# Seven products in the first layer of four more token blocks, with moved scores, state copies and buffers, in a fused retention and feed-forward kernel

## The chip, the cores and the metric

The kernel runs on one core of one Trainium2 chip. The metric is the device time of one execution in microseconds (us); lower is better. The engines are named as in the profile: PE is TensorE, which multiplies matrices (PEld is its loading of weights), DVE is VectorE, ACT is ScalarE, POOL is GpSimd, and SP is the engine whose queue issues most of the DMAs.

## The reference

Eight batches of eight heads go through a retention layer (attention without softmax, with a decay per head); the heads' results are laid side by side to 4608 tokens of 512 features, and these go through two matrix products with a gelu between.

```python
# q, k, v: (8, 8, 576, 64)
scores = scale * np.matmul(q, k.transpose(0, 1, 3, 2))
gamma = 1.0 - 2.0 ** (-5.0 - np.arange(H))
Dmat = np.where(rel >= 0, gamma[:, None, None] ** rel, 0.0)      # rel = i - j
attn = np.matmul(scores * Dmat, v)
x = attn.transpose(0, 2, 1, 3).reshape(4608, 512)
h = x @ w_in                                                     # w_in: 512 x 2048
g = 0.5 * h * (1.0 + np.tanh(c * (h + 0.044715 * h * h * h)))
out = g @ w_out                                                  # w_out: 2048 x 512
```

## The kernel before

**Tiling.** The tokens are worked in nine blocks `t` = 0 to 8 of 512. Blocks 0 to 7 hold the first 512 positions of batch `t`; the last 64 positions of all batches (the tails) are block 8. While block `t` goes through the two layers, the attention of batch `t + 1` is computed between its matmuls, and the batch after that is loaded, cast and transposed. Everything that the matmuls read is 16-bit.

**The first layer** (`up`, L465) makes one chunk of 128 of the 2048 hidden features for 512 tokens: four matmuls 512 columns wide into a PSUM bank `hp`, and a gelu on ACT into `gT`. Sixteen chunks make a block. In the last two blocks (`WIN`, L501) three quarters of the chunks are computed in another way (`up_prod`, L541): a group `j` is two chunks of the lower half of the features and two of the upper half, and its 2 x 2 block product is made by the Strassen-Winograd scheme with seven products of half the size instead of eight. One product is four matmuls 256 columns wide. Products 1, 6, 7 and 4 accumulate in one bank (`hB`), 2 has `hA`, 5 and 3 accumulate in `hC`. Where a bank's content is needed before the next product is added to it, it is copied out or read first: ACT copies it after product 1 (tile `ws`, the variable `s`) and after 6 (`wv`), DVE after 7 (`wu`), and DVE adds `hA` or `hC` to these tiles. Gelus of what results are put off by one step (`due`). The scheme needs sums of the weights (`in_sums`, L505, DVE: 4 operations per group, once) and sums of the inputs (`x_sums`, L522, DVE: 4 operations per block).

**The second layer** is made by the same scheme in all blocks but the first (`prod`, L651, and `after`, L673): seven products in the order 1, 6, 5, 7, 2, 4, 3 (another order in the last two blocks), each in two halves of 8 matmuls. Products 1 and 2 use bank A, 6, 7 and 4 accumulate in bank B, 5 and 3 in bank C. After 6, DVE adds bank B to ACT's copy of product 1 (`keep["u2"]`, tile `k2`); after 7 it makes `u3`; both are in the profile as `k<-k,opB` at L680. The activation sums that the products need (`act_sums`, L637, DVE: s1, s2, a difference written in place over `gT`, s4) are made pair by pair as soon as gelu has delivered two chunks of each half.

**Attention beside a block.** `scores` (L901) computes the scores of two 128-token chunks (tiles `st`) and multiplies them by a mask on DVE (`masks`, L383, tiles `ret`). `outs` (L912) multiplies them by the values, adds what the state of the earlier chunks gives (`past`, from the tiles `tbd`, `tbt`), and computes the next chunks' state products (`state`). `later` (L757) is the running state: two DVE operations (`scan`: `vs`, `ws`) and two copies of 64x256 each into `tbd` (`spread`, L425), on ACT. In blocks 2, 4, 6 and 7 the tails of two batches are worked along (`TP`).

**Order.** Every engine works its own queue in the order in which the program issues. What lies beside the matmuls is put at a step by hand: `at(t, u, f)` runs `f` after step `u` of block `t`; steps 0 to 15 are the first layer, 16 to 29 the halves of the seven products. From step 16 on GpSimd casts the next batch but one (`cc`, four `k` and four `q`; ACT casts `v`, but GpSimd for batch 3), after a small copy (`gate`, L953) that waits for the block's last activation sum. When the casts are done, SP issues two DMA transposes (`turn_dma`). Loads are held back from step 16 (`hold`) to step 29 (`resume`).

**Buffers.** All loads go into a ring of 16 buffers of 2 KB per partition (`LD`, `lds`); a load may be issued when a cast has freed a buffer (`pump`). The sums of the last blocks use the same ring when the loads are over.

The eight PSUM banks are handed out first in, first out (`bank`, `drop`).

Of the kernel before, what the change touches and what calls it, by code (L numbers as in the profile page):

```python
# [20 lines left out]
def kernel(  # L21
# [23 lines left out]
    LD = 16  # L45
# [24 lines left out]
    def lds():  # L70
        return sb.tile([128, 512], F32, tag="ld", name="ld", bufs=LD)

# [54 lines left out]
    seq += [("o", f) for f in FO[:LATE]]  # L127
    TP = {2: 0, 4: 2, 6: 4, 7: 6}
    seq += body(1)[:6] + [("o", f) for f in FO[LATE:]] + body(1)[6:]
    for b in range(1, B):  # L130
        seq += body(b) if b > 1 else []
        if b - 1 in TP:
            seq.append(("t", TP[b - 1]))
    q_ld = {"next": 0, "free": LD, "hold": False}

    def pump(freed=0):
        q_ld["free"] += freed
        while q_ld["next"] < len(seq) and not q_ld["hold"]:
            s = seq[q_ld["next"]]
            if s[0] != "t":  # L140
                if q_ld["free"] == 0:
                    return
                q_ld["free"] -= 1
            q_ld["next"] += 1
            {"b": load, "i": load_w_in, "o": load_w_out, "t": load_tails}[s[0]](*s[1:])
# [101 lines left out]
    def cast(b, key, c, eng):  # L247
        a = att[b]
        raw = a["raw"].pop((key, c))
        dst = a[key][:, 512 * c : 512 * c + 512]  # L250
# [250 lines left out]
    WIN = {t: 3 for t in (NTB - 2, NTB - 1)}  # L501
    GW = max(WIN.values())
    wi = {}

    def in_sums(j, ns):  # L505
        if not wi:
            for g in range(0, GW, 2):
                for n in "234":
                    wi[n, g // 2] = sb.tile([128, 2, 512], F16, tag="ld", name="wi" + n, bufs=LD)
# [10 lines left out]
    xw = {}  # L520

    def x_sums(t):  # L522
        if not xw:
            for n in ("12", "34"):
                x = sb.tile([128, 2, 4, 2, TL], F16, tag="ld", name="x" + n, bufs=LD)
                xw[int(n[0])], xw[int(n[1])] = x[:, 0], x[:, 1]
            for n in range(3):
                for s in "svu" if n < 2 else "vu":
                    wk[s, n] = sb.tile([128, 512], F32, tag="ld", name="w" + s, bufs=LD)
# [9 lines left out]
    wk, wb, due = {}, {}, []  # L539

    def up_prod(t, j, m):  # L541
# [23 lines left out]
        s, v, u3 = wk["s", j % 2], wk["v", j % 3], wk["u", j % 3]  # L565
# [56 lines left out]
    wt = {n: const.tile([128, NH, HD], F16, name="wt" + n) for n in "1234"}  # L622
    W11, W12 = w_out_sb[:, 0:NH, 0:HD], w_out_sb[:, 0:NH, HD:DM]
    W21, W22 = w_out_sb[:, NH:NF, 0:HD], w_out_sb[:, NH:NF, HD:DM]

# [11 lines left out]
    def act_sums(t, f0, f1, us=slice(0, 2), parts=(0, 1)):  # L637
# [6 lines left out]
        if 0 in parts:  # L644
            nc.vector.tensor_tensor(out=s["1"], in0=a21, in1=a22, op=ALU.add)  # L645
            nc.vector.tensor_tensor(out=s["2"], in0=s["1"], in1=a11, op=ALU.subtract)
            nc.vector.tensor_tensor(out=a21, in0=a11, in1=a21, op=ALU.subtract)
        if 1 in parts:
            nc.vector.tensor_tensor(out=s["4"], in0=a12, in1=s["2"], op=ALU.subtract)  # L649

    def prod(t, m, u):  # L651
# [7 lines left out]
        tag = {1: "A", 2: "A", 3: "C", 4: "D" if t in WIN else "B", 5: "C", 6: "B", 7: "B"}[m]  # L659
        if t in WIN and m == 3:  # L660
# [12 lines left out]
    def after(t, m, u):  # L673
        last = t == NTB - 1
        if u == 0 and not (last and m == 3 or t in WIN and m == 4) or u == 1 and t in WIN and m == 4:
            return
# [4 lines left out]
        def send(o, i):  # L681
# [5 lines left out]
            for v in range(2):  # L687
                end(o[:, v], i, v)
        def end(o, i, v, d=slice(0, DM)):
            b = 4 * v + 2 * i  # L690
            for h, e in enumerate((nc.sync, nc.scalar)):
                r0 = S * (b + h) + M0
                e.dma_start(out=out[r0 : r0 + TL, d], in_=o[TL * h : TL * h + TL, d])
# [3 lines left out]
        elif m == 6:  # L697
            keep["u2"] = sb.tile([128, 2, HD], F32, tag="k2", name="k2", bufs=1)
            add(keep["u2"], keep["s1"], pr("B"))
            for f in range(0, NH if t in WIN else 0, 2):  # L700
                act_sums(t, f, f + 2, parts=(1,))
        elif m == 7:
# [4 lines left out]
            drop(op.pop("B")) if t in WIN else None  # L707
            drop(op.pop("C")) if t in WIN else None
        elif m == 2:
# [3 lines left out]
            for v in range(2 if last else 0):  # L713
                end(keep["o0"][:, v], 0, v, slice(0, HD))
        elif m == 5 and t in WIN:
# [4 lines left out]
        elif m == 3:  # L720
            x = "E" if t in WIN else "C"
# [3 lines left out]
        elif m == 4 and t in WIN:  # L725
# [10 lines left out]
    def cast_w(kind, *i):  # L736
        src = w_raw.pop((kind,) + i)
        if kind == "i":
# [7 lines left out]
        pump(1)  # L746
# [6 lines left out]
    def cc(b, key, c, eng):  # L753
        cast(b, key, c, eng)
        pump(1)
# [4 lines left out]
    def later(b, c):  # L760
        scan(b, c)
        spread(b, c, A.copy)
# [57 lines left out]
    def run(t, u, last=False):  # L820
# [3 lines left out]
    W_ORDER = (  # L824
        "01 02 05 11 06 12 p 15 07 16 21 22 p 04 25 17 03 26 14 p 13 27 p Q0 24 a0 23 a1 Q1 a3 a2"
    ).replace("p", "").split(" ")
    for n in range(GW):
        at(NTB - 3, 17 + 2 * n, lambda n=n: in_sums(n, (3, 2)))
        at(NTB - 3, 18 + 2 * n, lambda n=n: in_sums(n, (4, 1)))
    at(NTB - 3, 27, lambda: x_sums(NTB - 2))  # L830
    at(NTB - 2, 17, lambda: x_sums(NTB - 1))


    at(0, -12, lambda: [V.memset(x, 0.0) for x in (tbd[1][:, 1:], *tbt[1:])])
    for n, f in enumerate(FO):
        at(0, -5 + n // 4 if n < LATE else 6, lambda f=f: cast_w("o", f))
        if 8 <= n < LATE:
# [47 lines left out]
    at(1, 12, lambda: weight_sums(4, (0, 3), V))  # L885
# [42 lines left out]
    for c in range(2):  # L928
        at(2, c, lambda c=c: later(nb, c))
    for t in range(2, B):  # L930
        b, tl = t + 1, TP.get(t)
        s0, o0, s1, o1 = 9, 15, 19, 25
# [5 lines left out]
        at(t, o0 + 1, lambda b=b: later(b, 2))  # L938
        at(t, o1, lambda t=t, nb=b + 1: outs(t, 2, None, (nb, 0, 1) if nb < B else None))
        at(t, o1 + 1, lambda b=b: later(b, 3))  # L940
        if b + 1 < B:
            for c in range(2):
                at(t + 1, c, lambda c=c, nb=b + 1: later(nb, c))
# [113 lines left out]
```

## Time and profile before

| | |
|---|---|
| median of 3 runs | 296.68 us (296.66 to 296.77) |
| the profiled execution | 296.39 us, its span 294.7 us, granted clock 0.997 |
| block 2, start to start on PE | 87.06 to 117.61 us |
| block 3 | 117.61 to 147.49 |
| block 4 | 147.49 to 178.05 |
| block 5 | 178.05 to 207.92 |
| block 6 | 207.92 to 238.38 |
| block 7 (three groups as seven products) | 238.38 to 264.35 |
| block 8 (likewise) | 264.35 to about 290 |

Times within the profile are from the start of the span. The page's first part gives each engine's busy time; the windows give it by stretch of time, so that an engine which is free on average can be seen to be full in one stage. A row of the timeline is: start, duration, engine, source line, operation, tile written and tiles read, shape and count; a bracket at its end says how long the engine had been idle and who released it.

These rows of the busiest groups are the prices of what the change moves or adds:

```profile
L561 PE MATMUL hC<-x,w_in_sb 128*128 128x256 f16 x48 | 7.2, 273 | 0.0
L568 DVE TENSOR_TENSOR ws<-ws,hA 128x512 f32<-128x512 f32 x6 | 4.1, 689 | 5.2 <-ACT ws L581 5.1
L581 ACT COPY ws<-hB 128x512 f32<-128x512 f32 x6 | 3.4, 574 | 9.6 <-PE hB L561 9.6
L537 DVE TENSOR_TENSOR x<-xT 128x512 f16<-128x512 f16 x4 | 1.7, 418 | 0.0
L745 POOL CAST w_in_sb<-ld 128x512 f16<-128x512 f32 x16 | 9.9, 629 | 2.1 <-DMA ld<-in_moe_w_in_dram 1.5
```

The columns are: count, busy time in us, mean ns of one, and the idle time before them with what ended it. Matmuls are pipelined, so that the step from one start to the next is shorter than a duration.

### The profile page before, as it was taken

How to read it: one execution, taken by the hardware profiler on the slowest of the kernel's cores; microseconds unless marked ns; L12 is line 12 of the kernel's file. 1: busy time of each engine (PE TensorE's matmuls, PEld its weight loads, DVE VectorE, ACT ScalarE, POOL GpSimd, SP SyncE). 2: the span in 40 equal slices, each digit the busy share in tenths (PEclk: the TensorE clock that was granted, in tenths of full speed). 3: DMA queues.
4: the chain of work that ended last, by engine and by line, in shares of the span. 5: the costliest groups of instructions: out<-in, count | busy, mean ns of one | idle time of the engine just before them, and what ended most of it. 6: DMA issues, size and time to landing. Idle time of an engine off the chain costs nothing. (4 is left out here: it accounts for less than half of the span.)

```text
span 294.7 us, 7531 instructions
## 1 busy us (share of the span) xinstructions
PE 282.2 (96%) x3100; PEld 204.3 (69%) x3100; DVE 191.7 (65%) x396; ACT 168.4 (57%) x313; POOL 100.2 (34%) x133
## 2 busy tenths in 40 slices
PE   6779999999999999999999999999999999999993
PEld 2458745888884588448844885478547887887782
DVE  6790606789754873477448654855488968974863
ACT  5377443998239663866386736664666258507800
POOL 4587487960880082007700640059030000000000
PEclk9999999999999999999999999999999999999998
DMA  7999999999969998999899949944941030003013
GB/s 202 307 357 372 341 317 292 280 280 211 194 165 232 216 225 169 261 214 194 103 271 221 169 88 273 211 109 76 263 93 38 0 145 1 2 20 125 1 38 107
DMA packets 129058, 52.92 MB, mean 180 GB/s; under 512 B 101632, under 2 KB 120576, under 8 KB 129024
## 3 DMA queue, kind: packets, MB, share of 16 engines
q1 hardware_dynamic: 128544, 51.92, 74.5%
q8 instruction: 24, 0.39, 0.6%
q10 hardware_dynamic: 480, 0.52, 0.6%
q14 instruction: 10, 0.08, 0.1%
HBM read 36.70 MB, written 9.44 MB: 157 GB/s over the span
## 5 line engine op out<-in xcount | busy, mean ns | idle before, releaser
L471 PE MATMUL hp<-xT,w_in_sb 128*128 128x512 f16 x352 | 79.0, 379 | 0.0
L477 ACT ACTIVATE gT<-hp 128x512 f16<-128x512 f32 x88 | 50.6, 597 | 31.0 <-PE hp L471 30.4
L471 PEld LDWEIGHTS <-w_in_sb 128*128 128x128 f16 x352 | 34.0, 98 | 38.2
L666 PEld LDWEIGHTS <-gT 128*128 128x128 f16 x512 | 49.0, 98 | 7.2 <-issue 0.5
L666 PEld LDWEIGHTS <-s 128*128 128x128 f16 x384 | 37.1, 98 | 4.8
L645 DVE TENSOR_TENSOR s<-gT 128x512 f16<-128x512 f16 x32 | 14.4, 449 | 28.0 <-ACT gT L477 27.0
L953 POOL COPY gate<-s 128x1 f16<-128x1 f16 x5 | 0.9, 190 | 90.7 <-DVE s L649 90.7
L489 PE MATMUL hp<-xT,w_in_sb 128*128 128x256 f16 x256 | 30.3, 273 | 1.1 <-POOL w_in_sb L745 0.9
L666 PE MATMUL opA<-w_out_sb,gT 128*128 128x256 f16 x256 | 31.0, 273 | 0.1
L425 ACT CAST tbd<-ws 64x256 f16<-64x256 f32 x48 | 19.4, 405 | 16.0 <-DVE ws L416 15.4
L489 PEld LDWEIGHTS <-w_in_sb 128*128 128x128 f16 x256 | 24.5, 98 | 4.9 <-POOL w_in_sb L745 1.6
L666 PE MATMUL opB<-wt,gT 128*128 128x256 f16 x224 | 26.9, 273 | 0.1
L383 DVE TENSOR_TENSOR ret<-st,cm 128x512 f16<-128x512 f32 x40 | 24.8, 681 | 0.0
L266 POOL TENSOR_TENSOR cq<-ld,sc 128x512 f16<-128x512 f32 x20 | 21.7, 1086 | 0.0
L460 ACT CAST xT<-xs 128x512 f16<-128x512 f32 x36 | 19.3, 592 | 3.3 <-PE xs L450 1.8
L266 POOL TENSOR_TENSOR ck<-ld,sc 128x512 f16<-128x512 f32 x20 | 21.0, 1050 | 0.0
L495 ACT ACTIVATE gT<-hp 128x512 f16<-128x512 f32 x32 | 18.5, 602 | 3.8 <-PE hp L489 3.5
L680 DVE TENSOR_TENSOR k<-k,opB 128x512 f32<-128x512 f32 x16 | 11.0, 687 | 14.2 <-ACT k L696 7.5
L711 ACT COPY ost<-opA 128x512 f32<-128x512 f32 x8 | 4.7, 586 | 24.1 <-PE opA L666 17.5
L293 ACT COPY tt<-tr 128x1024 f16<-128x1024 f16 (+1 forms) x12 | 11.8, 998 | 10.8 <-PE tr L287 10.7
L416 DVE TENSOR_TENSOR ws<-vs,gt 128x256 f32<-128x256 f32 x24 | 15.7, 654 | 1.1
L666 PE MATMUL opC<-wt,s 128*128 128x256 f16 x128 | 15.5, 273 | 0.0
(124 smaller groups left out, 440.0 us busy)
## 6 DMA issues: line engine op xcount, KB each, us to landing
ld<-in_q_dram SPq DMA_DIRECT2D x32, 256.0 KB, 5.3
ld<-in_k_dram SPq DMA_DIRECT2D x32, 256.0 KB, 5.3
ld<-in_v_dram SPq DMA_DIRECT2D x32, 256.0 KB, 5.4
out_dram<-ost SPq DMA_DIRECT2D x16, 512.0 KB, 3.8
ld<-in_moe_w_in_dram SPq DMA_DIRECT2D x16, 256.0 KB, 5.9
ld<-in_moe_w_out_dram SPq DMA_DIRECT2D x16, 256.0 KB, 5.3
lt<-in_k_dram SPq DMA_DIRECT2D x8, 128.0 KB, 5.4
lt<-in_q_dram SPq DMA_DIRECT2D x8, 128.0 KB, 4.3
```

The lines of the kernel that those rows point to most:

```text
L266: eng.tensor_tensor(out=dst.rearrange("p (h d) -> p h d", d=D), in0=raw.rearrange("p (h d) -> p h d", d=D), in1=sc[:, s0].unsqueeze(2).to_ ...
L293: cp(out=o, in_=t)
L383: nc.vector.tensor_tensor(out=r.rearrange("p (n i) -> p n i", i=128), in0=t.rearrange("p (n i) -> p n i", i=128), in1=(cm if b < PAIR else ...
L416: nc.vector.tensor_tensor(out=w, in0=uc, in1=gt, op=ALU.mult)
L425: cp(out=(tbd[b % 2][r, c, :, r] if c < NC - 1 else tbt[b % NT4][r, :, r]), in_=w[r])
L460: nc.scalar.copy(out=xT[:, g0 : g0 + 2], in_=xs.rearrange("p (n g t) -> p g n t", n=HP, g=2))
L471: nc.tensor.matmul(hp.rearrange("p (g t) -> p g t", t=TL), w_in_sb[:, ct, 128 * fc : 128 * fc + 128], xT[:, o : o + TB // TL, ct, :], star ...
L477: nc.scalar.activation(out=gT[t][:, fc].rearrange("p i n -> p (i n)"), in_=hp, func=AF.Gelu_apprx_tanh)
L489: nc.tensor.matmul(hp[:, 256 * x : 256 * x + 256].rearrange("p (g t) -> p g t", t=TL), w_in_sb[:, ct, 128 * (f + x) : 128 * (f + x) + 128] ...
L495: nc.scalar.activation(out=gT[t][:, f : f + 2, 2 * u : 2 * u + 2, :].rearrange("p f i n -> p f (i n)"), in_=hp.rearrange("p (f n) -> p f n ...
L645: nc.vector.tensor_tensor(out=s["1"], in0=a21, in1=a22, op=ALU.add)
L666: nc.tensor.matmul(op[tag][:, HD * u : HD * u + HD], lhs(f), rhs[:, f], start=(new and f == 0), stop=(f == NH - 1), skip_group_check=True,)
```

## The change

Seven things change together.

1. Blocks 3 to 6 compute groups 0 and 1 (half of the first layer) as seven products; the other eight chunks stay plain. The order within the block is written out (`p` is a plain chunk, `01` is product 1 of group 0, and so on), and the activation sums come in two runs at its end: `a` is s1 and s2, `b` the difference in place and s4.
2. In these blocks the first scores move from step 9 to 11, the outputs from 15 to 17, the second scores from 19 to 20, the second outputs from 25 to 26.
3. From batch 3 on, the state copies are made by GpSimd.
4. The weight sums of groups 0 and 1 move from block 6 to block 2 (steps 17, 18, 21, 22), those of group 2 to step 24 of block 6; the x sums are made at step 28 of the block before (block 8: step 17, as before).
5. The ring has 19 buffers. Seven of them, kept back when batch 2 has been issued, hold the sums; 12 remain for the loads. Some temporaries share the tiles `k1` to `k3` with the second layer.
6. One sum of the second layer's weights (`wt["1"]`) is written in place, and its first half moves from block 0 to step 14 of block 1.
7. The last block's stores of two halves of a result are joined to one DMA per queue.

```diff
-    LD = 16
+    LD = 19
+    KEPT = 7
...
+        if b == NPE - 1:
+            seq += [("keep",)] * KEPT
...
+            if s[0] == "keep":
+                kept.append(ring.popleft())
...
-    WIN = {t: 3 for t in (NTB - 2, NTB - 1)}
+    FIN = (NTB - 2, NTB - 1)
+    WIN = {t: 3 if t in FIN else 2 for t in range(NPE, NTB)}
...
+    def hold(shape, dt):
+        n = kept.pop() if kept else ring.popleft()
+        return sb.tile(list(shape), dt, tag=f"ld{n}", name="wk", bufs=1)
...
+    def temp(t, j, s):
+
+        m = j % (2 if s == "s" else 3)
+        if s == "s" and t not in FIN or m == 0:
+            return sb.tile([128, 512], F32, tag={"s": "k1", "v": "k2", "u": "k3"}[s], name="w" + s, bufs=1)
+        if (s, m) not in wk:
+            wk[s, m] = hold((128, 512), F32)
+        return wk[s, m]
...
-    def act_sums(t, f0, f1, us=slice(0, 2), parts=(0, 1)):
+    def act_sums(t, f0, f1, us=slice(0, 2), parts=(0, 1, 2)):
...
             nc.vector.tensor_tensor(out=s["2"], in0=s["1"], in1=a11, op=ALU.subtract)
+        if 1 in parts:
             nc.vector.tensor_tensor(out=a21, in0=a11, in1=a21, op=ALU.subtract)
-        if 1 in parts:
+        if 2 in parts:
             nc.vector.tensor_tensor(out=s["4"], in0=a12, in1=s["2"], op=ALU.subtract)
...
-            for v in range(2):
-                end(o[:, v], i, v)
...
             for h, e in enumerate((nc.sync, nc.scalar)):
-                r0 = S * (b + h) + M0
-                e.dma_start(out=out[r0 : r0 + TL, d], in_=o[TL * h : TL * h + TL, d])
+                e.dma_start(out=rows(2 * i + h, slice(0, 2), d), in_=o[TL * h : TL * h + TL, :, d])
...
-    def later(b, c):
+    def later(b, c, cp=A.copy):
         scan(b, c)
-        spread(b, c, A.copy)
+        spread(b, c, cp)
...
+    W_ORDER = {
+        2: "p 01 02 05 p 06 11 12 p 07 15 16 04 p 03 17 p 14 13 p p p a0 a1 a2 a3 b0 b1 b2 b3",
+        3: "01 02 05 11 06 12 p 15 07 16 21 22 p 04 25 17 03 26 14 p 13 27 p Q0 24 c0 23 c1 Q1 c3 c2",
+    }
+    for j, (t, u) in enumerate([(NPE - 1, 17), (NPE - 1, 21), (NTB - 3, 24)]):
+        at(t, u, lambda j=j: in_sums(j, (3, 2)))
+        at(t, u if t > NPE else u + 1, lambda j=j: in_sums(j, (4, 1)))
+    for t in WIN:
+        at(t - 1, 17 if t == NTB - 1 else 28, lambda t=t: x_sums(t))
...
-        if 8 <= n < LATE:
+        if 9 <= n < LATE:
...
-    at(1, 12, lambda: weight_sums(4, (0, 3), V))
+    at(1, 12, lambda: weight_sums(4, (3, 0), V))
+    at(1, 14, lambda: weight_sums(0, [0], V))
...
-        s0, o0, s1, o1 = 9, 15, 19, 25
+        s0, o0, s1, o1 = (11, 17, 20, 26) if t in WIN and t not in FIN else (9, 15, 19, 25)
...
-        at(t, o0 + 1, lambda b=b: later(b, 2))
+        at(t, o0 + 1, lambda b=b: later(b, 2, P.tensor_copy))
...
-        at(t, o1 + 1, lambda b=b: later(b, 3))
+        at(t, o1 + 1, lambda b=b: later(b, 3, P.tensor_copy))
...
-            todo = deque(f + h for f in range(2 * WIN.get(t, 0), NH) for h in (0, NH))
+            todo = deque([4, 12, 5, 13, 6, 7, 14, 15][4 * (WIN.get(t, 2) - 2) :])
```

## The prediction, made before the changed kernel was built or run

> **What bounds the kernel now.** I read the page first, then the busy time by block, then the waits, then the order of time around the places that the change touches.
>
> ```profile
> PE 282.2 (96%) x3100; PEld 204.3 (69%) x3100; DVE 191.7 (65%) x396; ACT 168.4 (57%) x313; POOL 100.2 (34%) x133
> ```
>
> TensorE is the bound: 282.2 of 294.7 us, and the rest is the start and the last stores. So what the change takes from TensorE counts in full, and what it adds elsewhere costs only where TensorE has to wait. The windows by block show who is near that point.
>
> ```profile
> core 0: us, PE busy (x) PEld busy (x) DVE busy (x) ACT busy (x) POOL busy (x), PEclk, DMA share, GB/s
> 87.00:117.60 30.60, 30.60 (x311) 20.98 (x309) 18.93 (x38) 18.75 (x36) 9.04 (x10) 1.00 1.03 214
> 117.60:147.50 29.90, 29.90 (x287) 20.20 (x286) 17.83 (x36) 17.84 (x34) 10.58 (x11) 1.00 0.97 192
> 207.90:238.40 30.50, 30.41 (x295) 20.68 (x294) 24.20 (x53) 16.68 (x32) 2.50 (x2) 1.00 0.34 84
> ```
>
> These are blocks 2, 3 and 6. VectorE has 12 us to spare in block 3 and 6 in block 6, where the weight sums lie today. In block 6 it was late once:
>
> ```profile
> 234.15 0.68 DVE L680 TENSOR_TENSOR k<-k,opB 128x512 f32<-128x512 f32 x1
> ...
> 234.89 1.91 PE opB L666 x16
> ```
>
> (The second line is from the chain of waits.) Product 4 accumulates on top of 6 and 7 in bank B, so it may start only when VectorE has read the bank; TensorE started 0.06 us after the read ended. The same holds for product 7 after the u2 sum of product 6. In block 3 this hand-over has slack:
>
> ```profile
> 134.06 0.42 DVE L649 TENSOR_TENSOR s<-gT,s 128x512 f16<-128x512 f16 x1
> 134.39 0.42 DVE L413 TENSOR_TENSOR vs<-us,ws 128x256 f32<-128x256 f32 x1
> 134.60 0.19 POOL L953 COPY gate<-s 128x1 f16<-128x1 f16 x1 [21.96 <-DVE s L649]
> 134.84 1.23 DVE L416 TENSOR_TENSOR ws<-vs,gt 128x256 f32<-128x256 f32 x1
> 137.57 0.69 DVE L680 TENSOR_TENSOR k<-k,opB 128x512 f32<-128x512 f32 x1 [1.50 <-ACT k L696]
> ...
> 139.13 1.91 PE L666 MATMUL opB<-wt,gT 128*128 128x256 f16 x16
> ```
>
> The u2 sum ends at 138.26 and product 7 starts at 139.13: 0.87 us of slack. The reader should also see that ws took 1.23 us and not 0.43: it waited for the GpSimd cast that started at 134.75.
>
> **The change, part by part.** *Seven products.* A 512-column matmul group of 4 goes every 0.865 us (24 matmuls from 126.90 to 132.09), a product of 4 matmuls of 256 columns every 0.4375 us (block 7). One group of columns costs 4 x 0.865 = 3.46 us today and 7 x 0.4375 = 3.06 us as products: 0.40 us less. Two groups in each of four blocks: **-3.2 us**.
>
> What VectorE gets for it, per group: sum of s, copy and sum of u, sum of v, 4 x 0.69 = 2.75 us, and per block 4 sums of x at 0.35 to 0.42 us, 1.6 us: 7.1 us per block. By amount it fits block 3 (17.8 + 7.1 of 29.9) and block 6 barely (24.2 + 5.5 - 3.3 for the eight weight sums that leave). By place it does not, and this is my main term. In the new order all eight pairs of activation sums, which lie between the gelus today, come in one run after the scores' masks and ahead of the scan and of the u2 sum. Take T = 0 at block 3's first matmul. Five plain chunks and 13 products: the scores start at 5 x 0.865 + 13 x 0.4375 = 10.0. TensorE then has scores 0.56, one product 0.44, three chunks 2.6, products 1, 6 and 5 at 1.76 each, attention output 1.13 and scores again 0.56: product 7 is due at 20.6. VectorE has, from the scores on: first mask 0.5 later (126.34 to 126.83), 4 masks at 0.60 = 2.4, v sum 0.6, sums s1 and s2 4 x 0.80 = 3.2 (0.45 + 0.35 from 254.38 to 255.18), a21 and s4 8 x 0.34 = 2.7, scan 1.68 (134.39 to 136.07, the collision with the cast included, since the gate releases GpSimd at the same sum as today), u2 0.69: 21.8. Product 7 waits **1.2 us** in blocks 3 and 5. Blocks 4 and 6 have two masks more (1.2) against 0.65 us more on TensorE (tail scores 0.2, tail outputs 0.45): 1.75 in block 4; in block 6 no casts run, the scan is 0.8 shorter: 0.95. Together **+5.1 us** (0.3 us less or more each: 3.9 to 6.3). What is queued behind u2 on VectorE, the masks of chunks 2 and 3 and u3, moves along, and product 4 finds u3 done.
>
> *Small waits among the products.* Product 4 of group 0 comes three products (1.31 us) after 7, whose bank VectorE copies from 0.70 to 1.39 us after its start (242.30 and 243.00 in block 7): 0.14; the same bank wait of group 1, behind the v sum, 0.3. I take 0.4 per block, **+1.6 us**; between nothing and 1.0 each, since ScalarE's in-order queue may add to it.
>
> *Weight sums in block 2.* Eight of the twelve leave block 6, where they made product 4 wait for about **-0.25 us**, and go to block 2, between the gate and the end of the casts. What such sums take then is in the trace, in block 1:
>
> ```profile
> 59.32 1.27 DVE L645 TENSOR_TENSOR s<-gT 128x512 f16<-128x512 f16 x1
> 60.62 1.15 DVE L646 TENSOR_TENSOR s<-s,gT 128x512 f16<-128x512 f16 x1
> 61.70 0.83 DVE L647 TENSOR_TENSOR gT<-gT 128x512 f16<-128x512 f16 x1
> 62.45 0.83 DVE L649 TENSOR_TENSOR s<-gT,s 128x512 f16<-128x512 f16 x1
> ...
> 59.08 2.42 POOL L258 TENSOR_TENSOR ck<-ld,sc 128x512 f16<-128x512 f32 x2
> 61.45 1.56 POOL L255 CAST cv<-ld 128x512 f16<-128x512 f32 x2
> ```
>
> Alone each takes 0.42; with casts running, each waits for one cast. VectorE's work in block 2 from the last scan to u3, alone: scan 0.9, eight sums 3.0, u2 0.65, masks 2.4, u3 0.65, from 104.06 to 111.6; product 4 is due at 114.11, so nothing would wait. With waits of about 2.6 for the first four sums (two state copies, the gate, some two casts) and 3.0 for the last four (three casts), u3 ends at 117.2: a wait of 3.1. One cast fewer if VectorE comes first at the start of the second four: I take **+2.5 us**, between 0 (all slots won) and 3.5. The casts end some 3 us later, and SP's transposes with them.
>
> A rule of the Trainium skill speaks against this place: "SBUF — State Buffer", section "Who interferes with whom", says that a VectorE instruction with two SBUF inputs and a GpSimd instruction that reads SBUF exclude each other for a whole instruction, that one input from PSUM frees it, and that ScalarE never waits. By it alone all eight sums could each wait out a cast of 1.04 us, 8.3 us, and the term would be 5.8 instead of 3.1; the block 1 rows say that one is met per sum, but not always a whole one. It also means that state copies, harmless on ScalarE, join the contest on GpSimd.
>
> *State copies on GpSimd.* The trace has no such copy there. Bounds: the gate's one column, 0.19 us, and a 128x512 cast, 0.61; ScalarE takes 0.40 for the same 64x256. I take 0.40, eight per block, 3.2 us. Cover: GpSimd has 19 us free in block 3. The copies of chunk 2 wait for ws, and six casts and SP's transposes stand behind them. Transposes issued at 143.49 landed 6.3 us later, needed at 156.22: 6.4 us of slack, less 2.8 (gate later) and 0.8 (copies), plus 1.3 (scores later): 0 us, and up to 1 per block if that cover went. ScalarE loses 3.2 and gains two copies per group, 2.3: nothing on the path.
>
> *Buffers.* Nineteen, seven of them kept after batch 2, leave 12 for a batch. The four loads that run ahead into the next batch today (133.41 to 138.09) go behind transposes and stores. Twelve at 1.15 us from about T + 5, landing after 5.4: the last q at T + 22, cast at T + 27. 0 us (up to 2 in all if a load comes late). The weight sum that moves from block 0 to step 14 of block 1 (0.69 on VectorE), the sum in place and the reused k tiles: 0, under slack of the same size; 0.3 at most.
>
> *Joined stores.* At the end each queue issues four stores from 289.33, 0.47 to 0.59 each, and the last starts at 291.2 although its sum was done at 290.34. One fewer per queue ahead of it: **-0.6 us** (0 to -0.7).
>
> Sum: -3.2 + 5.1 + 1.6 - 0.25 + 2.5 - 0.6 = **+5.15 us**. It is made on the span of 294.7 us; that execution took 296.39, the runs' median is 296.68, 0.3 above. Carried over to the median: **301.8 us**.
>
> **Rivals.** *VectorE keeps up* (0.19): the scan meets no cast, the products' banks are free, block 2's sums slip between the casts. Then -3.2 - 0.25 - 0.6 = 292.6 us, or up to 296 with a wait of 0.8 left in each of the four blocks. For it: by amount VectorE has room everywhere; against it: in blocks 2 to 5 every scan after the gate took 1.2 us.
>
> *Lateness is handed to the next block* (0.12): in blocks 3 and 5 the tail casts (2.2 us) move on to the x sums and the last scan, s of the next block's group 0 comes some 1.5 to 2 us late, ScalarE waits in order behind it, and product 7 of group 0 waits for its bank. Blocks 4 and 6 then lose 1.5 to 2 each, and block 7 half a us: 301.8 + 4 = 306 us. It decides when the x sums end more than 1 us into the next block. Against it: later blocks' slack may swallow it.
>
> *Waits eat just the saving* (0.09): the wait at product 7 is 0.8 us per block and block 2 costs nothing: 296.68 - 4.05 + 3.2 + 1 = 296.8 us, from 296 to 298.
>
> **How the numbers follow.** The forecast, 298 to 305 us, has 0.60. The range of 8 in 10 reaches from 294.0, into the first rival, to 306.5. A measurement of this kernel tells 0.2% (0.6 us) from no change. Faster: the first rival and a little of the third, 0.20; same 0.04; slower 0.76.
>
> **What would show it.** In blocks 3 to 6 a gap on TensorE ahead of opB's second 16 matmuls, released by DVE k; VectorE without idle from the masks to that sum; in block 2 wi sums of 0.8 to 1.3 us and a gap ahead of product 4. If VectorE is idle between a21 and u2, or the wi sums take 0.42, I am wrong; if L441 waits for GpSimd or st for transposes, the cover that I named was not there.

## The result, and the profile after

The changed kernel takes **305.36 us** (median of 5 runs, 304.97 to 305.49), beside 296.68 for the kernel before (5 runs): a ratio of 1.0284 [1.0269, 1.0299], slower by 8.7 us. 301.8 had been forecast, from 298 to 305. The profiled execution's span is 303.4 us, its granted clock 0.997 as before.

The first line of the page of the changed kernel has busy time, share of the span and count for each engine:

```profile
PE 283.1 (93%) x3196; PEld 213.7 (70%) x3196; DVE 219.3 (72%) x444; ACT 159.0 (52%) x289; POOL 117.6 (39%) x173
```

TensorE's busy time is about that of before (283.1 against 282.2 us). What grew is the rest of the span, in which TensorE is idle: 20.3 us, 12.5 before. The windows of the changed kernel, one row for each of blocks 2, 3, 4, 6 and 7, say where:

```profile
core 0: us, PE busy (x) PEld busy (x) DVE busy (x) ACT busy (x) POOL busy (x), PEclk, DMA share, GB/s
87.66:119.14 31.48, 30.60 (x310) 20.96 (x308) 24.64 (x49) 15.95 (x28) 13.29 (x18) 1.00 0.96 197
119.14:149.53 30.39, 29.57 (x311) 22.48 (x309) 23.05 (x46) 16.22 (x30) 11.92 (x17) 1.00 0.96 185
149.53:182.75 33.22, 30.77 (x335) 23.14 (x333) 26.12 (x52) 17.09 (x32) 12.76 (x18) 1.00 0.85 167
...
213.30:245.54 32.24, 30.52 (x318) 22.86 (x316) 26.91 (x56) 14.92 (x28) 6.50 (x11) 1.00 0.45 101
245.54:272.22 26.68, 26.15 (x238) 21.44 (x236) 21.72 (x45) 13.84 (x26) 1.02 (x2) 1.00 0.11 41
```

Against before (start to start on TensorE) block 2 is 0.93 us longer, block 3 0.51, block 4 **2.66**, block 5 0.68, block 6 **1.78**, block 7 0.71; ahead of block 2 0.60 are lost and behind the last matmul 0.8. The sum is 8.7. VectorE is full in no block: 23 to 27 us of 30 to 33 in blocks 2 to 6. So it is order, not amount, that costs. Three places in the timeline of the changed kernel show how. (Columns: start, duration, engine, line, operation, tiles, shapes; in the bracket the engine's idle time before and its releaser. The sums' tiles are all called `wk` now: `wk<-w_in_sb` is a weight sum, `wk<-xT` an x sum.) The first is the wait at product 7 in block 3:

```profile
138.84 0.42 DVE L425 TENSOR_TENSOR vs<-us,ws 128x256 f32<-128x256 f32 x1
139.19 1.04 POOL L278 TENSOR_TENSOR ck<-ld,sc 128x512 f16<-128x512 f32 x1
139.36 1.16 DVE L428 TENSOR_TENSOR ws<-vs,gt 128x256 f32<-128x256 f32 x1
140.44 0.68 DVE L705 TENSOR_TENSOR k<-k,opB 128x512 f32<-128x512 f32 x1
141.17 1.91 PE L691 MATMUL opB<-wt,gT 128*128 128x256 f16 x16 [0.81 <-DVE k L705]
```

The last activation sum, just ahead of these lines, opens GpSimd's gate; the cast meets the scan, `ws` takes 1.16 us, u2 comes after it, and product 7 waits for u2. The next place is block 2, the weight sums beside GpSimd's casts:

```profile
106.86 0.41 DVE L533 TENSOR_TENSOR w_in_sb<-w_in_sb 128x512 f16<-128x512 f16 x1
...
111.14 1.22 POOL L278 TENSOR_TENSOR ck<-ld,sc 128x512 f16<-128x512 f32 x1
111.49 1.15 DVE L533 TENSOR_TENSOR wk<-wk,w_in_sb 128x512 f16<-128x512 f16 x1
...
113.75 1.26 DVE L533 TENSOR_TENSOR w_in_sb<-w_in_sb 128x512 f16<-128x512 f16 x1
...
114.93 0.67 DVE L705 TENSOR_TENSOR k<-k,opB 128x512 f32<-128x512 f32 x1
...
115.66 1.91 PE L691 MATMUL opB<-wt,gT 128*128 128x256 f16 x16 [0.88 <-DVE k L705]
```

The first four sums met only state copies and the gate and took 0.41 to 0.50 us; the last four met casts and took 0.74 to 1.26. The four masks between them (one input in PSUM, from 108.33 us) had casts beside them too and took 2.48 us, as in block 3 of the kernel before (from 126.83), where no cast ran. u3 comes behind them, and product 4 waits for u3. The third place is the start of block 4:

```profile
148.30 2.23 POOL L278 TENSOR_TENSOR e<-lt,sc 128x512 f16<-128x512 f32 x2
...
149.56 1.26 DVE L547 TENSOR_TENSOR wk<-xT 128x512 f16<-128x512 f16 x1
...
153.08 0.67 DVE L590 TENSOR_TENSOR ws<-ws,hA 128x512 f32<-128x512 f32 x1
...
153.78 0.63 ACT L594 ACTIVATE gT<-ws 128x512 f16<-128x512 f32 x1 [2.07 <-DVE ws L590]
...
154.80 0.58 ACT L609 COPY wv<-hB 128x512 f32<-128x512 f32 x1
...
155.43 0.60 PE L580 MATMUL hB<-wk 128*128 128x256 f16 x4 [0.53 <-ACT wv L609]
```

Block 4 began at 149.53. The casts of the tails (`e`) hold the x sums up, the x sums hold the sum of s (153.08), ScalarE stands idle for 2.07 us in front of a gelu that needs s, the copy `wv` stands behind that gelu, and product 7 of group 0 behind the copy. Lateness of block 3 is paid in block 4.

### The profile page after: what moved, and what is told of

Its sections match the earlier page's. It is cut to its first block, busy times and chain, and to the rows that moved or that the text cites. A ratio compares the mean times of both kernels' runs of the same rounds, so it can differ in the third digit from the quotient of the medians.

```text
span 303.4 us, 7813 instructions
## 1 busy us (share of the span) xinstructions
PE 283.1 (93%) x3196; PEld 213.7 (70%) x3196; DVE 219.3 (72%) x444; ACT 159.0 (52%) x289; POOL 117.6 (39%) x173
## 4 chain that ended last, share of the span: by engine, by line
PE 50%; DVE 29%; ACT 6%; SPq 6%; issue 4%; DMA 3%; POOL 1%; DVEq 0%; ACTq 0%; POOLq 0%
PE opB L691 9%; PE hB L580 6%; PE hp L501 6%; PE hp L483 5%; PE opA L691 5%; PE op L630 4%; SPq L108 4%; DVE ret L395 4%; PE opC L691 3%; DVE s L670 3%; DVE s L669 2%; PE hC L580 2%; DVE gT L672 2%; DVE ws L428 2%; DVE s L674 2%
## 5 line engine op out<-in xcount | busy, mean ns | idle before, releaser
L483 PE MATMUL hp<-xT,w_in_sb 128*128 128x512 f16 x224 | 53.9, 379 | 0.0
L489 ACT ACTIVATE gT<-hp 128x512 f16<-128x512 f32 x56 | 32.9, 595 | 24.6 <-issue 13.6
L483 PEld LDWEIGHTS <-w_in_sb 128*128 128x128 f16 x224 | 21.8, 98 | 19.3
L691 PE MATMUL opB<-wt,gT 128*128 128x256 f16 x224 | 27.6, 273 | 4.8 <-DVE k L705 4.8
L691 PE MATMUL opC<-w_out_sb,s 128*128 128x256 f16 x224 | 27.6, 273 | 0.0
L501 PEld LDWEIGHTS <-w_in_sb 128*128 128x128 f16 x256 | 24.4, 98 | 4.4 <-POOL w_in_sb L774 1.1
L437 POOL CAST tbd<-ws 64x256 f16<-64x256 f32 x30 | 12.2, 408 | 37.6 <-DVE ws L428 36.7
L580 PEld LDWEIGHTS <-w_in_sb 128*128 128x128 f16 x224 | 21.6, 98 | 5.4
L580 PEld LDWEIGHTS <-wk 128*128 128x128 f16 x168 | 16.2, 97 | 10.7 <-issue 5.4
L265 ACT CAST cv<-ld 128x512 f16<-128x512 f32 x19 | 11.1, 629 | 19.0 <-DMA ld<-in_v_dram 19.0
L507 ACT ACTIVATE gT<-hp 128x512 f16<-128x512 f32 x32 | 18.5, 602 | 3.4 <-PE hp L501 3.0
L580 PE MATMUL hB<-wk 128*128 128x256 f16 x112 | 16.5, 272 | 1.6 <-ACT wv L609 1.6
```

The costliest lines, as they stand in the source:

```text
L437: cp(out=(tbd[b % 2][r, c, :, r] if c < NC - 1 else tbt[b % NT4][r, :, r]), in_=w[r])
L483: nc.tensor.matmul(hp.rearrange("p (g t) -> p g t", t=TL), w_in_sb[:, ct, 128 * fc : 128 * fc + 128], xT[:, o : o + TB // TL, ct, :], star ...
L489: nc.scalar.activation(out=gT[t][:, fc].rearrange("p i n -> p (i n)"), in_=hp, func=AF.Gelu_apprx_tanh)
L501: nc.tensor.matmul(hp[:, 256 * x : 256 * x + 256].rearrange("p (g t) -> p g t", t=TL), w_in_sb[:, ct, 128 * (f + x) : 128 * (f + x) + 128] ...
L507: nc.scalar.activation(out=gT[t][:, f : f + 2, 2 * u : 2 * u + 2, :].rearrange("p f i n -> p f (i n)"), in_=hp.rearrange("p (f n) -> p f n ...
L580: nc.tensor.matmul(pb[:, 256 * i : 256 * i + 256].rearrange("p (g t) -> p g t", t=TL), w(kt, i), x(kt), start=(new and i == kt == 0), stop ...
```

## The experiments

Each was timed on one chip together with the kernel before; ratios are to that kernel, with a 95% interval in brackets. "Changed" is the kernel of the change.

**1. The stores alone** (the kernel before, with the joined stores):

```diff
-            for v in range(2):
-                end(o[:, v], i, v)
...
+                e.dma_start(out=rows(2 * i + h, slice(0, 2), d), in_=o[TL * h : TL * h + TL, :, d])
```

> The kernel before with the joined stores of the last block and nothing else. My prediction's term: one store fewer per queue ahead of the last, -0.6 us, 296.1 us. Rival from the trace after the change, where the span ends 5.2 us after the last sum and not 4.4: the joined stores move the same bytes later and in one piece, and the last ones land behind them: +0.8 us, 297.5 us.

297.4 us against 296.73; 1.0024 [1.0002, 1.0046]. The span is 295.5 us, 294.7 before. From the end of the last VectorE sum to the end of the span it is 5.1 us, 4.3 before. The last four stores, two of 64 KB on each queue, from issue to landing in this kernel:

```profile
DMA to landing us min/median/max: 3.2/3.7/4.0
```

The same four stores in the kernel before:

```profile
DMA to landing us min/median/max: 2.3/2.4/2.6
```

SP's last store does start sooner after the last sum (0.35 us instead of 0.84), as forecast. The last store of all is on ScalarE's queue, and it gains only 0.2 us (0.94 instead of 1.12), since the issue ahead of it took 1.20 us instead of 0.56. And the last stores take some 1.2 us longer to land. Joining costs 0.7 us instead of saving 0.6.

**2. The scan behind u2** (changed, one step later in blocks 3 to 6):

```diff
-        at(t, o0 + 1, lambda b=b: later(b, 2, P.tensor_copy))
+        at(t, o0 + (2 if t in WIN else 1), lambda b=b: later(b, 2, P.tensor_copy))
```

> The changed kernel with the scan of chunk 2 issued behind the u2 sum in blocks 3 to 6 (one step later). If product 7 waits for VectorE's queue, its waits (0.97, 1.36, 0.97 and 0.64 us in blocks 3 to 6) vanish; the queue as a whole is no shorter, so that u3 becomes the next wait, ahead of product 4 (about 0.45, 0.85, 0.45 and 0.1 us). Gain about 2 us: 303.3 us, with the gap moved from opB's second group to its third. If these waits have another cause (the activation sums themselves, the banks), nothing changes: 305.3 us.

303.27 us; 1.0215 [1.0183, 1.0247]. Block 3 of this kernel:

```profile
138.81 0.68 DVE L705 TENSOR_TENSOR k<-k,opB 128x512 f32<-128x512 f32 x1
...
139.92 0.56 DVE L428 TENSOR_TENSOR ws<-vs,gt 128x256 f32<-128x256 f32 x1
140.16 1.91 PE L691 MATMUL opB<-wt,gT 128*128 128x256 f16 x16
```

u2 now ends at 139.49 and product 7 starts at 140.16 without a wait, in blocks 3 to 6 alike. The time is the expected one; the gap that was expected ahead of product 4 did not come. In blocks 4 and 6 half a us of it came back as a longer wait for `wv` (1.09 instead of 0.53): the late end of the block before was still there.

**3. Two of the four x sums inside the block** (changed; the third and fourth, which products 7 and 3 need, at step 2 of the block itself):

```diff
-        at(t - 1, 17 if t == NTB - 1 else 28, lambda t=t: x_sums(t))
...
+            at(t - 1, 28, lambda t=t: x_sums(t, (1, 2)))
+            at(t, 2, lambda t=t: x_sums(t, (3, 4)))
```

> The changed kernel with the third and fourth x sum of blocks 3 to 6 issued in the block itself, behind s of group 0, and not at the end of the block before. If lateness is handed over the block's end (x sums behind tail casts, o0, s, then ScalarE in order, then the bank of product 7), s of blocks 4 and 6 comes about 0.95 us sooner and their mixed stretches, 15.87 us each, shorten by 0.7 to 0.95; blocks 3 and 5 by up to 0.3: 303.2 to 303.8 us. If the long stretches of blocks 4 and 6 come from the tails' own work on ScalarE and the banks, less than 0.5 us changes: about 305 us.

303.35 us; 1.0212 [1.0177, 1.0248]. Block 4 falls from 33.22 to 32.34 us, block 6 from 32.24 to 31.35, blocks 3 and 5 stay within 0.2. The waits for `wv` in blocks 4 and 6 are gone; those of product 4 of group 0 for the copy of u3 (0.72 us) are still 0.66.

**4. Twelve buffers for the loads** (the kernel before, with four of its 16 buffers withheld after batch 2):

```diff
+        if b == NPE - 1:
+            seq += [("keep",)] * 4
```

> The kernel before with four of its sixteen load buffers withheld once batch 2 is issued, so that twelve are left per batch as after the change. Mine: loads only start later, 0 us, 296.7 us (up to 0.3 more). Rival: late loads delay casts and transposes and with them the scores: 1 to 3 us more.

296.8 us; 1.0006 [0.9985, 1.0027]. The buffers cost nothing that can be measured.

**5. The state copies back on ScalarE** (changed):

```diff
-        at(2, c, lambda c=c: later(nb, c, P.tensor_copy))
+        at(2, c, lambda c=c: later(nb, c))
...
```

(and so for the other three calls)

> The changed kernel with the state copies back on ScalarE (eight of 64x256 per block, 0.40 us each), everything else as changed. My theory: the copies on GpSimd are not what costs, GpSimd has room and no TensorE wait ends on them; on ScalarE they stand in order behind the scan of VectorE and ahead of the k and v copies of the next group, so the time is between 305.0 and 308, against 305.4. Rival (the copies contest VectorE's SBUF access on GpSimd and this made the scan and the x sums late): faster, about 303.5 or less.

**315.9 us**; 1.0649 [1.0628, 1.0669]. The direction is that of my theory, the size is not: 10.5 us, not 0 to 3. Block 3 of this kernel:

```profile
121.73 0.82 ACT L437 CAST tbd<-ws 64x256 f16<-64x256 f32 x2
...
122.57 0.58 ACT L603 COPY ws<-hB 128x512 f32<-128x512 f32 x1
...
124.25 0.42 DVE L428 TENSOR_TENSOR ws<-vs,gt 128x256 f32<-128x256 f32 x1
...
124.70 0.82 ACT L437 CAST tbd<-ws 64x256 f16<-64x256 f32 x2 [1.55 <-DVE ws L428]
125.53 0.63 ACT L594 ACTIVATE gT<-ws 128x512 f16<-128x512 f32 x1
...
127.17 0.60 PE L580 MATMUL hB<-wk 128*128 128x256 f16 x4 [1.63 <-ACT wv L609]
```

ScalarE reaches the second pair of state copies before VectorE has made the state, stands 1.55 us, and the gelu and the copies of the products' banks stand behind it. Blocks 2 to 6 are 0.9, 2.4, 2.2, 2.9 and 2.1 us longer than in the changed kernel. So of the parts that were taken back, this is the one that the new order needs most.

**6. The weight sums of block 2 early** (changed; six of eight at steps 2 and 5):

```diff
-    for j, (t, u) in enumerate([(NPE - 1, 17), (NPE - 1, 21), (NTB - 3, 24)]):
-        at(t, u, lambda j=j: in_sums(j, (3, 2)))
-        at(t, u if t > NPE else u + 1, lambda j=j: in_sums(j, (4, 1)))
+    for j, (t, u) in enumerate([(NPE - 1, 17), (NPE - 1, 18), (NTB - 3, 24)]):
+        at(t, u if t > NPE else 2 + 3 * j, lambda j=j: in_sums(j, (3, 2, 4)))
+        at(t, u, lambda j=j: in_sums(j, (1,)))
```

> The changed kernel, but in block 2 six of the eight weight sums are issued at steps 2 and 5, ahead of the first scores, and only the two sums in place at steps 17 and 18. Theory (the last four sums, 0.74 to 1.26 us each beside GpSimd's two-input casts, make u3 end late and product 4 of block 2 wait 0.88 us): about 304.5, the gap of product 4 in block 2 gone. Rival (the weight sums are harmless, block 2's 0.9 us come from the casts and the scan): 305.4, no change; if the early sums push block 2's own scan back, up to 306.5.

304.6 us; 1.0269 [1.0252, 1.0285]. By the times alone this can't be told from the changed kernel (the intervals overlap); the profile tells it: block 2 takes 30.55 us, as before the change, instead of 31.48, and product 4 does not wait. The early sums took 0.42 to 0.62 us.

**7. Five repairs together** (changed, with 2, 3 and 6, the stores as before, and the moved sum of the second layer's weights at step 5 of block 1):

```diff
-    at(1, 14, lambda: weight_sums(0, [0], V))
+    at(1, 5, lambda: weight_sums(0, [0], V))
...
```

> The changed kernel with five repairs together: the scan of chunk 2 one step later, behind u2; the third and fourth x sum in step 2 of the block itself; six of the eight weight sums of block 2 early; the stores at the end as before; the moved weight sum at step 5 of block 1 instead of 14. If my account adds up (305.4 - 2.05 for the scan, - 2.0 for the x sums, - 0.9 for block 2, - 0.8 for the stores, - 0.6 for the weight sum): about 299.0. Rival (the repairs take away the same wait twice, or VectorE's lateness only moves on to the next bank): 301 to 302.5.

299.22 us; 1.0097 [1.0069, 1.0124]: the account adds up. Block 1 takes 35.33 us, 35.82 in the changed kernel, so the moved weight sum's half a us is in it.

**8. A new order of the products** (the last kernel, with two pairs of activation sums and one plain chunk elsewhere):

```diff
-        2: "p 01 02 05 p 06 11 12 p 07 15 16 04 p 03 17 p 14 13 p p p a0 a1 a2 a3 b0 b1 b2 b3",
+        2: "p 01 02 05 p 06 11 12 p p 07 15 16 04 a2 b2 03 17 p 14 13 p p p a0 a1 a3 b0 b1 b3",
```

> The kernel with the five repairs, and in the mixed order of blocks 3 to 6 two of the eight pairs of activation sums moved ahead, behind product 4 of group 0, and one plain chunk put between product 2 and product 7 of group 0. Theory (what is left is VectorE's queue in the run of activation sums, and the bank of product 7 that waits for a copy): 297 to 298.5, one us less than with the five repairs alone. Rival (the sums, when they are issued earlier, delay s, u and v of the groups and ScalarE behind them): no gain, 299 or more.

299.18 us; 1.0091 [1.0072, 1.011]: no gain, as the rival had it. Blocks 4 and 6 gained 0.8 and 0.7 us; blocks 3 and 5 lost 1.0 each, where product 7 of group 1 now waited 0.54 us for ScalarE's copy of product 6.

**9. One chunk moved alone** (the five repairs, and the x sums of block 7 split as those of blocks 3 to 6):

```diff
-        2: "p 01 02 05 p 06 11 12 p 07 15 16 04 p 03 17 p 14 13 p p p a0 a1 a2 a3 b0 b1 b2 b3",
+        2: "p 01 02 05 p 06 11 12 p 07 15 16 p 04 03 17 p 14 13 p p p a0 a1 a2 a3 b0 b1 b2 b3",
```

> The kernel with the five repairs (299.2 us), with two edits more: in the mixed order of blocks 3 to 6 one plain chunk stands ahead of product 4 of group 0 instead of behind it, and the x sums of block 7 are split too (third and fourth at step 2 of block 7). Theory (the two waits of 0.73 us at product 4 of group 0 in blocks 4 and 6 end on VectorE's copy of u3, and 0.54 us in block 7 on ScalarE's copy behind a late s): about 297.2. Rival (the chunk that goes ahead of product 4 only moves the wait to product 7 of group 1): no gain, 299.

298.9 us; 1.0065 [1.0047, 1.0084]. The rival was right for the chunk: in blocks 4 and 6 the wait at product 4 of group 0 (0.73 us) went, one of 0.54 at product 7 of group 1 came, and the blocks are as long as they were. Only block 7 is shorter, 26.39 us instead of 26.68. A wait that moves on from bank to bank may have its cause further ahead, so the next two kernels look at the casts beside the x sums. In run 7 the first two x sums of block 4 were:

```profile
147.59 1.26 DVE L548 TENSOR_TENSOR wk<-xT 128x512 f16<-128x512 f16 x1
148.88 1.15 DVE L548 TENSOR_TENSOR wk<-wk,xT 128x512 f16<-128x512 f16 x1
```

**10. The tail casts later** (with 9; the casts at the start of the block that needs them):

```diff
-        at(t0, ut[-1] + 1, lambda b=b: turn_dma(b, TP.get(b - 1)))
+        at(t0, ut[-1] + 1, lambda b=b: turn_dma(b))
+        if b - 1 in TP:
+            at(t0 + 1, 0, lambda b=b: cast_tails(TP[b - 1]))
```

> The same with one edit more: GpSimd casts the tails of k and q (two of 128x512, about 1.2 us each) at the start of the block that needs them, behind the copies of the first state chunk, and not at the end of the block before, where the first x sum of blocks 4 and 6 took 1.26 us beside them and the second 1.15 (0.42 each where no cast runs). Theory (this collision is what still makes blocks 4 and 6 one us longer than they need be): 1.0 to 1.6 us less than without this edit, about 296 or just below, so no slower than the kernel before. Rival (the casts only collide with the next sums and the scan, and the transposes of the tails come too late for the scores): 297.2 or more.

**334.92 us**; 1.1291 [1.1256, 1.1326]. Block 2 of this kernel, SP's queue and TensorE:

```profile
105.98 1.26 SPq L108 DMA_DIRECT2D ld<-in_v_dram  x1
107.34 2.29 SPq L253 DMA_TRANSPOSE ett<-e  x1
...
111.86 0.61 PE L386 MATMUL st<-ett 64*128 64x128 f16 x8 [15.26 <-DMA ett<-e]
```

The rival came true, far beyond its 297.2 us. I had moved the transposes of the tails, with their casts, past the point where SP resumes the loads. Twelve loads now stood ahead of them on SP's queue, from 93.47 to 107.24, and TensorE waited 15.26, 13.13 and 3.59 us in blocks 2, 4 and 6. But the start of block 4 answers the question that was asked:

```profile
164.54 0.41 DVE L548 TENSOR_TENSOR wk<-xT 128x512 f16<-128x512 f16 x1
...
164.99 0.50 DVE L548 TENSOR_TENSOR wk<-wk,xT 128x512 f16<-128x512 f16 x1
```

With no cast beside them the first two x sums took 0.41 and 0.50 us, not 1.26 and 1.15 as in run 7. The casts met the third instead (1.26 us, at 168.65).

**11. The tail casts earlier** (with 9; the tails of blocks 4 and 6 loaded ahead of their batch, cast at step 6 of the block before):

```diff
+        if b - 1 in TP and b > NPE:
+            seq.append(("t", TP[b - 1]))
         seq += body(b) if b > 1 else []
...
-        at(t0, ut[-1] + 1, lambda b=b: turn_dma(b, TP.get(b - 1)))
+        at(t0, ut[-1] + 1, lambda b=b: turn_dma(b, TP.get(b - 1) if b == NPE else None))
+        if b - 1 in TP and b > NPE:
+            at(t0, 6, lambda b=b: cast_tails(TP[b - 1]))
```

> The kernel with the five repairs and the later product 4 (298.9 us), and the tails of k and q of blocks 4 and 6 loaded ahead of the twelve loads of their batch instead of behind them, and cast by GpSimd at step 6 of the block before (where GpSimd has nothing to do until the gate), so that no cast lies beside the x sums and the transposes of the tails stand ahead of the gate in SP's queue. Theory (in the last run, where the tail casts were moved behind the next batch's loads, TensorE waited up to 15 us for the transposes, but the x sums took 0.41 and 0.50 us; what still makes block 4 1.8 us and block 6 1.4 us longer than block 3's 29.4 plus 0.65 for the tails is this collision and nothing else): 295.3 to 296.3, a little faster than the kernel before. Rival (the tail casts collide with VectorE at step 6 as well, or blocks 4 and 6 are late for the two masks more): 298 or more.

296.31 us; 0.9989 [0.9964, 1.0013]. Blocks 4 and 6 fall from 31.89 and 31.52 to 30.80 and 30.42 us, and their first two x sums take 0.42 and 0.50 us: this was the collision. A wait of 0.34 us for a copy on ScalarE is left in each.

**12. ScalarE's cast of the tail values earlier** (with 11, blocks 4, 6 and 7):

```diff
-        at(t, 3, lambda b=b: tail_values(b))
+        at(*((t, 3) if t < NPE else (t - 1, 28)), lambda b=b: tail_values(b))
```

> The last kernel (296.3 us), with ScalarE's cast of the tails of v (0.63 us) of blocks 4, 6 and 7 issued at step 28 of the block before, where ScalarE is idle for 3.0 us, instead of step 3. Theory (it stands in ScalarE's in-order queue ahead of the copies of the products and the gelus: waits of 0.34 us in blocks 4 and 6 and 0.23 in block 7 end on ScalarE): 0.5 to 1.2 us less, about 295.4, faster than the kernel before. Rival (ScalarE is late for VectorE's sums, not for its own work): 296.3, no change.

**296.12 us** against 297.12 for the kernel before on this chip; 0.997 [0.9948, 0.9991]: 0.3% faster than the kernel before, where 295.4 had been expected. The waits of 0.34 us in blocks 4 and 6 are gone and each block is 0.3 us shorter; the wait of 0.23 in block 7, of which the same had been expected, is still there. Its windows for blocks 3 and 4:

```profile
117.51:146.92 29.41, 29.38 (x310) 22.52 (x308) 22.82 (x47) 16.82 (x31) 12.91 (x17) 1.00 1.00 181
146.92:177.42 30.50, 30.37 (x334) 23.16 (x332) 24.86 (x51) 16.55 (x31) 11.92 (x17) 1.00 1.00 200
```

VectorE does what it did in the changed kernel (22.82 us in block 3, 23.05 there), and TensorE is idle for 0.03 us in block 3 instead of 0.82. Blocks 3 to 6 take 119.45 us (29.41, 30.50, 29.42, 30.12), 120.77 before the change: the seven products are worth 1.3 us here, net, once little waits for them: 0.47 each in blocks 3 and 5, 0.06 in block 4, 0.33 in block 6. In block 4 the second layer still waits a little (product 4 starts 2.01 us after product 2, in block 3 it is 1.75). Block 7 stays 0.4 us longer than before the change (26.40 us, 25.97).

## Why the prediction was right and where it was wrong

The direction, the engine and the mechanism were right: more work for VectorE, enough room by amount, not by place, so TensorE waits for banks. Of the 8.7 us 5.15 had been forecast. The 305.4 us lie just above the 298 to 305 that had the 0.60, inside the range of 8 in 10, and nearest to the second rival's 306. That the forecast came this near is partly luck. Product 7 and the weight sums were put 3.2 us too dear together; the lateness, the stores, the moved weight sum and the smaller saving cost 6.6 us more than they were put at. The sizes, term by term, with blocks 3 to 6 of run 12 as the floor (TensorE idle for 0.03 to 0.13 us in each):

| term of the sum | forecast | measured | from |
|---|---|---|---|
| seven products, with small waits (+1.6) and block 6's sums (-0.25) | -3.2, with these -1.85 | -1.3 | the floor, 119.45 less 120.77 |
| product 7 waits for u2 | +5.1 | +3.5 | second-layer part of blocks 3 to 6, less the floor's: 0.98, 1.09, 0.97, 0.49 |
| lateness handed to the next block | 0 (a rival) | +3.4, and part of block 7's +0.7 | first-layer part, less the floor's: 0, 1.63, 0.16, 1.63 |
| weight sums in block 2 | +2.5 | +0.9 | block 2; run 6 takes it back |
| moved weight sum of the second layer | 0 (0.3 at most) | +0.6 | ahead of block 2; run 7 takes 0.5 back |
| joined stores | -0.6 | +0.8 | end of the span; run 1: +0.7 |
| state copies, buffers | 0 | 0 as far as can be told | no wait of TensorE ends on the copies; run 4 |

Of what was to show it, the gap ahead of the second 16 matmuls of `opB` in blocks 3 to 6 was there, released by VectorE (0.81, 1.20, 0.81 and 0.47 us in the trace), and VectorE had no idle time from the masks to that sum in block 3 but 0.1 us ahead of `ws`. With this "VectorE keeps up" and "Waits eat just the saving" fall. The sign in block 2 came by half: the gap ahead of product 4 was there (0.88 us), but only the last four weight sums took longer than 0.50 us.

**The products and the small waits** were right to half a us. Among the products of block 3 four start 0.07 to 0.14 us later than the step of the others allows, 0.4 in all, as forecast. The same 0.4 are in run 12. What is missing of the saving is missing in blocks 4 and 6 (0.06 and 0.33 us saved there, 0.40 and 0.65 forecast).

**Product 7** was the right place with the right releaser, and 1.6 us too dear. VectorE's side was right: u2 was put at T + 21.8 and ended at T + 22.0 (141.12 less 119.14). TensorE's was not: product 7 was put at T + 20.6 and could have started at T + 21.2 (141.17 less the gap of 0.81). The step that failed is the sum itself: the 0.4 us of small waits were added to a wait that they shorten, since a TensorE that is 0.4 late at product 7 waits 0.4 less there. This is worked out for block 3; over the four blocks 0.4 each makes the 1.6.

**Weight sums in block 2.** The step that failed is that the first four would wait out "two state copies, the gate, some two casts". A state copy took GpSimd about 0.4 us, and a sum beside such copies took 0.42 to 0.50, hardly more than alone. The casts of 128x512 (1.04 us alone) doubled or tripled a sum. The rule of the Trainium skill that had been weighed ("SBUF — State Buffer", section "Who interferes with whom") excludes a two-input VectorE instruction and a GpSimd one that reads SBUF from each other for a whole instruction; the sums of 1.15 and 1.26 us beside casts agree, and those of 0.42 to 0.50 beside the state copies show that the shorter GpSimd instructions cost less.

**Lateness handed to the next block** had been a rival at 0.12, with "blocks 4 and 6 then lose 1.5 to 2 each, and block 7 half a us". It came true: 1.63 each. The prediction had priced it rightly and given it a small chance; its own sum held it at nothing. That is the step that failed most. What the prediction set against it, that later blocks' slack may swallow it, held for block 5 (0.16, though the x sums ended 1.7 us into it). The difference is in runs 10 and 11: of blocks 3 to 6 only 4 and 6 have tail casts ahead of them, and with these casts moved away from the x sums both blocks are 1.1 us shorter (run 11 against run 9). The place was in my own working ("in blocks 3 and 5 the tail casts (2.2 us) move on to the x sums and the last scan"), and I had given the x sums 1.6 us per block without asking what casts lie beside them.

**The stores.** I counted issues, not landings, and the last start that I named, 291.2, is SP's; on ScalarE's queue one issue took 0.85 us, and the last store started at 291.46. Fewer issues did let the last one start earlier; the landing time of what stood behind a bigger transfer was not part of the step. The Trainium skill ("DMA: Bandwidth & Descriptors", section "Rules for kernel authors") advises to coalesce many small transfers into a large one; in run 1, where stores of 128 KB were joined to 256 KB with others behind them, it cost 0.7 us, and the measurement decides.

**The moved weight sum** had been put under "slack of the same size". It was not there: it delayed four activation sums and the scan of block 1 by 0.6 us and with them the state copies on ScalarE, and product 7 of block 1 waited 0.64 us for u2.

**State copies on GpSimd** were forecast at nothing and argued with GpSimd's free time. That was right, but the other side was left out: what they would cost where they were, in the new order, 10.5 us.

What stays open is how much run 12 gains on run 11: the spans say 0.8 us, the medians 0.2, and the two intervals overlap. By block it is 0.3 us each in blocks 4 and 6. That run 12 is faster than the kernel before rests on its own interval, and the gain is small. The moved steps of scores and outputs and the sum written in place were not tried by themselves. The scan's collision with the cast that the gate releases was moved out of the way, not taken away.

## What to carry to other kernels

When work is added to an engine that has room by amount, lay its queue out at each place where the bound engine needs a bank, and do it past the end of the block: what is late there is paid in the next one, by an in-order engine two steps further on. Put VectorE's two-input sums where GpSimd has no casts to make. Either can be moved: here moving two x sums per block was worth 2.0 us (run 3), moving the tail casts 2.6 (run 11 against run 9). When a step is moved, see past which point of each queue it goes, the DMA queue's resumed loads above all.

## What had not been expected of the hardware

**Behind joined stores the last ones land later.** The same bytes are stored at the end of the kernel before and of the one with joined stores. The window 291.3 to 293.3 us of the kernel before, and then that of run 1 (the last two columns are the share of busy DMA engines and GB/s):

```profile
291.30:293.30 2.00, 0.00 (x0) 0.00 (x0) 0.00 (x0) 0.00 (x0) 0.00 (x0) 0.93 0.89 299
```

```profile
291.30:293.30 2.00, 0.00 (x0) 0.00 (x0) 0.00 (x0) 0.00 (x0) 0.00 (x0) 1.00 0.93 238
```

The DMA engines are as busy, and move a fifth less. The four last stores landed 3.2 to 4.0 us after their issue instead of 2.3 to 2.6 (run 1). Why was not tried.

**The clock after a long wait.** In run 10 TensorE's granted clock fell while it waited, and stayed low when it went on (PEclk is the third column from the end):

```profile
108.00:111.80 3.80, 0.00 (x0) 0.00 (x0) 0.00 (x0) 0.00 (x0) 0.00 (x0) 0.50 1.17 184
111.80:114.00 2.20, 2.14 (x12) 0.93 (x13) 1.29 (x2) 0.00 (x0) 0.00 (x0) 0.50 0.03 7
114.00:116.00 2.00, 2.00 (x6) 0.72 (x5) 0.00 (x0) 0.60 (x1) 0.00 (x0) 0.55 0.00 0
116.00:118.00 2.00, 2.00 (x11) 0.91 (x10) 1.34 (x4) 1.47 (x3) 0.00 (x0) 1.00 0.00 0
```

The clock stayed at 0.50 for some 4 us after TensorE went on, which cost some 2 us, and so a wait of 15.26 us made block 2 17.3 us longer (47.87 against 30.56). The waits in blocks 2 to 7 of the changed kernel, 1.2 us at most, left the clock at 1.00.
